# Halved conversion steps for the second matrix, scalars in early pieces, and the last reload moved, in a fused attention and two-layer kernel

## The chip, the cores and the metric

The kernel runs on one core of a Trainium2 chip. The metric is the device time of one execution in microseconds (us). Five engines work side by side, each through its own stream of instructions in order: TensorE (PE, and PEld for its weight loads), VectorE (DVE), ScalarE (ACT), GpSimd (POOL) and SyncE (SP), which here only issues transfers. They wait for each other through semaphores.

## The reference

Attention over 4 batches of 8 heads, 768 positions, head size 64, with a causal window of 128 and the first 4 positions kept for all; then two dense layers with a squared ReLU between them.

```python
scores = scale * np.matmul(q, k.transpose(0, 1, 3, 2))
rel = pos[:, None] - pos[None, :]
keep = (pos[None, :] < n_sink) | ((rel >= 0) & (rel < window))
scores = np.where(keep, scores, -1000000000.0)
a = np.exp(scores - np.max(scores, axis=-1, keepdims=True))
a = a / (np.sum(a, axis=-1, keepdims=True) + 1e-09)
x = np.matmul(a, v)          # as 3072 tokens x 512
h = x @ w_in                 # 512 -> 2048
r = np.maximum(h, 0.0)
g = s * (r * r) + b          # two scalars
out = g @ w_out              # 2048 -> 512
```

Two scalars, `s` and `b`, stand between the layers. [...]

## The kernel before

**Numbers.** Every operand of a matmul is held as a high part in TensorE's reduced 32-bit format and a low part, the difference; three products stand for one. A 64-bit value is read as two 32-bit words, and `float_steps` (L228) makes a 32-bit float of them: ScalarE scales the low word (L235) and the high word (L236), VectorE shifts the high word left by three into a scratch tile (L237), merges the sign (L239) and adds the low word (L241). Each works on 128 lanes x 1024 elements.

**Stages.** Tokens come in eight chunks of 384 (`CH`), each a half of a batch. The first stage computes attention for chunk 0 (`first_slots`) and converts the first matrix. Then comes a long list of steps of the first layer, 16 values of f per chunk in four pieces each (`l1_steps`, L678; L692 is its matmul, L698 its ReLU, L700 stores it to memory). Between these steps other work is placed: each entry of `todo` (L1056 to L1059) has a due time in units of f, and the loop takes out the entries that are due before it traces the next piece. `second_slots` is attention for the second chunk, `attn_slots` that of the other six: `unit_a` makes scores (L339, L340), the masked minimum on VectorE (L344) and the exponential on ScalarE (L350); `unit_b` transposes (L363, L364) and splits into high (L368, ScalarE) and low (L369, VectorE); `unit_c` and `unit_d` make the output and divide by the sum (L405, L432 to L438). One stage has all matmul outputs in eight PSUM banks, which come free when VectorE or ScalarE has read them.

**The second matrix** has eight blocks q (`NP`), each two rows of 128 x 512. The second layer uses a scheme with seven products of half blocks (`products`, L803; its matmul is L817), so a block needs seven matrices: three of its quarters and four sums, which `w2_steps` (L712) makes: `float_steps`, then subtractions into T (L718), `t0_t2` for two more of them, `low` for the quarters' high and low parts (L721 and L718), a copy of T in high form (L734, ScalarE) and the low form (L718, 128 x 1024). `tc.keep_in_program_order` pins an instruction's place among other pinned ones on its engine; the rest is ordered by a planner with its own costs. Six blocks are converted early: `early_w2` (L740) yields 12 steps per block, one of them the load of the next raw block, and they get due times spread evenly over 94 values of f. Three of these are written to memory and come back later through `reload` (L760), a transfer issued by POOL. The last two blocks are converted in the last chunk's first-layer stage (`late_w2`, L1077), in four calls each, and a reload follows each four; one call is taken per value of f.

**The second layer** has 48 units: six groups of 512 tokens times eight blocks. `load` brings the stored ReLU of one block on SP, `prep` squares it (L785), applies the scalars and forms the seven left operands (L787 to L798), `products` multiplies. The loop loads three units ahead and prepares one ahead.

**The scalars.** `scalars` (L190) works on single elements per lane: sign, scaled copies and a square root of |s| by four rounds of Newton's method (L205 to L208). It is due at t2 = 10.8, when attention for the second chunk is nearly done. Its results are first read by L236 of the second matrix's conversion.

Of the kernel before, what the change touches and what calls it, by code (L numbers as in the profile page):

```python
# [8 lines left out]
F32 = mybir.dt.float32  # L9
F32R = mybir.dt.float32r  # L10
I32 = mybir.dt.int32
U32 = mybir.dt.uint32
U8 = mybir.dt.uint8
AF = mybir.ActivationFunctionType
ALU = mybir.AluOpType
# [19 lines left out]
EARLY, SPILL = 3, 3  # L35
HD = DM // 2
NP = NF // 2
# [4 lines left out]
LB, LC, LD, L2, LEAD, PIECES = 3, 5, 2, 2, 2, 4  # L42
# [3 lines left out]
def tile_kernel(ctx, tc, qT, kT, k0, v, vsk, n_sink, window, w1, w2, s, b, out):  # L46
    nc = tc.nc
# [21 lines left out]
    def kept_v(q, name, shape, dt=F32):  # L69
        return kept.tile(shape, dt, tag=f"v{q}", name=name)  # L70

    def kept_raw(name, shape=(P, 2, 2 * DM), dt=I32):
        return kept.tile(list(shape), dt, tag="raw", name=name)
# [40 lines left out]
    rel, rel1, low, upp, kix, snk, tmp, tm2 = (sc0[:, j, :] for j in range(8))  # L114
# [73 lines left out]
    root_ap, b1_ap, b2_ap, sgn_ap, up_ap, abs_ap, t1_ap, t2_ap = (sbu[:, j:j + 1] for j in range(8))  # L188

    def scalars():  # L190


        ts = nc.vector.tensor_scalar
        stt = nc.vector.scalar_tensor_tensor
        tc.keep_in_program_order(ts(out=sgn_ap, in0=s_ap, scalar1=0.0, scalar2=2.0, op0=ALU.is_ge, op1=ALU.mult))
        ts(out=sgn_ap, in0=sgn_ap, scalar1=1.0, scalar2=None, op0=ALU.subtract)
        ts(out=up_ap, in0=sgn_ap, scalar1=2.0 ** -111, scalar2=None, op0=ALU.mult)
        stt(out=b1_ap, in0=b_ap, scalar=1 / WUP, in1=sgn_ap, op0=ALU.mult, op1=ALU.mult)
        ts(out=b2_ap, in0=b1_ap, scalar1=2.0, scalar2=None, op0=ALU.mult)
        nc.vector.tensor_tensor(out=abs_ap, in0=s_ap, in1=sgn_ap, op=ALU.mult)  # L200
        ts(out=abs_ap, in0=abs_ap, scalar1=1 / WUP, scalar2=1e-36, op0=ALU.mult, op1=ALU.max)
        ts(out=root_ap.bitcast(I32), in0=abs_ap.bitcast(I32), scalar1=1, scalar2=None, op0=ALU.logical_shift_right)
        ts(out=root_ap.bitcast(I32), in0=root_ap.bitcast(I32), scalar1=0x1fbd1df5, scalar2=None, op0=ALU.add)
        for _ in range(4):
            nc.vector.reciprocal(out=t1_ap, in_=root_ap)  # L205
            nc.vector.tensor_tensor(out=t2_ap, in0=t1_ap, in1=abs_ap, op=ALU.mult)
            nc.vector.tensor_tensor(out=t2_ap, in0=t2_ap, in1=root_ap, op=ALU.add)
            ts(out=root_ap, in0=t2_ap, scalar1=0.5, scalar2=None, op0=ALU.mult)  # L208

# [13 lines left out]
    def scratch(name, dt=F32):  # L225
        return kept.tile([P, 2, DM], dt, tag="cs", name=name, bufs=2)

    def float_steps(raw, scratch, pin=lambda x: x, up=2.0 ** -111):  # L228


        lo, hi = raw[..., 0], raw[..., 1]
        t = []
        sc, ve = nc.scalar, nc.vector
        return [
            lambda: pin(sc.activation(lo, lo.bitcast(U32), AF.Copy, scale=2.0 ** -29)),  # L235
            lambda: pin(sc.mul(hi.bitcast(F32), hi.bitcast(F32), up)),  # L236
            lambda: pin(ve.tensor_scalar(out=t.append(scratch()) or t[0], in0=hi, scalar1=3, scalar2=None,  # L237
                                         op0=ALU.logical_shift_left)),
            lambda: pin(ve.scalar_tensor_tensor(out=t[0], in0=hi, scalar=-0x80000000, in1=t[0],  # L239
                                                op0=ALU.bitwise_and, op1=ALU.bitwise_or)),  # L240
            lambda: pin(ve.tensor_tensor(out=hi, in0=t[0], in1=lo, op=ALU.add))]  # L241

    def to_float(raw, t):
        for f in float_steps(raw, lambda: t):
# [433 lines left out]
    def l1_steps(k, before):  # L678

        tk = slice(k.c * CH, (k.c + 1) * CH)  # L680
        g = {}

        order = [(cc, wi, 0) for cc in range(NCC) for wi in range(2)] + [(cc, 0, 1) for cc in range(NCC)]
        n = len(order) // PIECES

        def l1(f, piece):
            if piece == 0:
                before(f)
                g["h"] = po("h")
            h = g["h"]  # L690
            for i, (cc, wi, xi) in list(enumerate(order))[piece * n:(piece + 1) * n]:
                nc.tensor.matmul(h[:, :CH], w_in(f, wi)[:, cc * P:(cc + 1) * P], k.x[xi][:, cc, :],  # L692
                                 start=(i == 0), stop=(i == len(order) - 1))
            if piece < PIECES - 1:
                return
            if f % 2 == 0:
                g["r"] = kept.tile([P, 2, CH], F32, tag="g", name="g", bufs=3)
            nc.scalar.activation(g["r"][:, f % 2], h[:, :CH], AF.Relu, scale=1.0 / WUP)  # L698
            if f % 2 == 1:
                nc.sync.dma_start(gs[f // 2][:, :, tk], g["r"])  # L700

        return [lambda f=f, piece=piece: l1(f, piece) for f in range(NF) for piece in range(PIECES)]

    wc, raw2 = {}, {}
    spilled = {q: dram.tile([P, 7, 2, HD], F32R, tag=f"wd{q}", name=f"wd{q}") for q in range(EARLY, EARLY + SPILL)}

    def load_w2(q, raw=None):
        raw = kept_raw(f"vraw{q}") if raw is None else raw
        nc.sync.dma_start(raw, w2[q])
        raw2[q] = raw.rearrange("p c (f t) -> p c f t", t=2)  # L710

    def w2_steps(q):  # L712

        pin = tc.keep_in_program_order
        wb, wt = wc[q]
        v = raw2[q][..., 1].bitcast(F32)
        T = scratch("vT").rearrange("p c (h f) -> p (c h) f", h=2)
        sub = lambda o, x, y: pin(nc.vector.tensor_tensor(out=o, in0=x, in1=y, op=ALU.subtract))  # L718

        def low(o, x):  # L720
            pin(nc.scalar.copy(o[:, :, 0], x))  # L721
            sub(o[:, :, 1], x, o[:, :, 0].bitcast(F32))

        def t0_t2():
            sub(T[:, 2], v[:, 1, HD:], T[:, 1])
            sub(T[:, 0], T[:, 2], v[:, 1, :HD])

        o2 = T.rearrange("p (a c) f -> p c a f", c=2)[:, 1]
        return float_steps(raw2[q], lambda: scratch("vt", I32), pin, up_ap) + [
            lambda: sub(o2, v[:, :, HD:], v[:, 0].rearrange("p (h f) -> p h f", h=2)),  # L730
            t0_t2,
            lambda: low(wb[:, 0:2], v[:, :, :HD]),
            lambda: low(wb[:, 2:3], v[:, 1:2, HD:]),
            lambda: pin(nc.scalar.copy(wt[:, :, 0], T)),  # L734
            lambda: sub(wt[:, :, 1], T, wt[:, :, 0].bitcast(F32))]

    def halves_of(t):
        return t[:, :3], t[:, 3:]

    def early_w2():  # L740

        order = [(EARLY + j, j) for j in range(SPILL)] + [(q, q) for q in range(EARLY)]
        yield lambda: load_w2(order[0][0])
        for n, (q, tag) in enumerate(order):
            t = kept_v(tag, f"v{q}", [P, 7, 2, HD], F32R)
            wc[q] = halves_of(t)
            steps = w2_steps(q)
            if n + 1 < len(order):
                steps.insert(9, lambda: load_w2(order[n + 1][0]))
            yield from steps  # L750
            if q in spilled:
                nc.sync.dma_start(spilled[q].bitcast(F32), t.bitcast(F32))
# [290 lines left out]
            weights(NP - 1, (i - 20) // 2)  # L1043
    first_cm.__exit__(None, None, None)
    early = early_w2()
    n_early = 12 * (EARLY + SPILL)
    k2, plain = second_slots(ORDER[1])
    chunks = [k, k2] + [new_chunk(c) for c in ORDER[2:]]
    rows = attn_slots(chunks[2:])
    steps = [f for j, c in enumerate(chunks) for f in l1_steps(c, before if j == 0 else lambda f: None)]  # L1050
    n_last = (NC_ - 1) * NF

    t1 = NF / len(plain)
    t2 = H * BLK * t1 - LEAD
    dt = (n_last - LEAD - t2) / len(rows)
    todo = [(max(t * t1 - LEAD, 0.3), f) for t, f in enumerate(plain)] + [(t2 - 2, constants3), (t2, scalars)]  # L1056
    todo += [(t2 + t * dt, f) for t, f in enumerate(rows)]
    todo += [(NF + (t + 0.5) * (n_last - LEAD - NF) / n_early, lambda: next(early)()) for t in range(n_early)]
    todo.sort(key=lambda x: x[0])  # L1059
    n = 0  # L1060
# [13 lines left out]
    reload, load, prep, products, n_units = second_layer(p2)  # L1074
    late = {}

    def late_w2(q, a, z):  # L1077
        if a == 0:
            late[q] = w2_steps(q)
        for f in late[q][a:z]:  # L1080
            f()

    todo = []
    for j in range(2):
        todo += [lambda q=NP - 2 + j, a=a, z=z: late_w2(q, a, z) for a, z in ((0, 2), (2, 5), (5, 9), (9, 11))]
        todo.append(lambda j=j: reload(EARLY + 1 + j))
    for m in range(n, len(steps)):
        steps[m]()
        if m % PIECES < PIECES - 1:
# [1 line left out]
        m = m // PIECES - n_last  # L1091
# [7 lines left out]
    for n in range(n_units):  # L1099
        if n + 1 < n_units:  # L1100
            prep(n + 1)
        if n + 3 < n_units:
            load(n + 3)
        products(n)
    p2_cm.__exit__(None, None, None)
    kept_cm.__exit__(None, None, None)
# [49 lines left out]
```

## Time and profile before

| what | us |
| --- | --- |
| median of 3 runs | 728.08 (727.44 to 730.79) |
| profiled execution | 726.22 |
| its span | 724.5 |
| PE busy | 696.1 (96%) |
| PEld busy | 659.1 (91%) |
| DVE busy | 575.6 (79%) |
| ACT busy | 531.7 (73%) |
| POOL busy | 130.5 (18%) |

The span is what the profile covers; the execution's own time adds 1.7 us around it. A busy time is the time in which an engine has at least one instruction in work. Matmuls are pipelined, so a shown end lies behind the start of the next one; weight loads stand end to end when nothing holds TensorE up. The times of one kernel in different executions differ by a few tenths of a per cent.

### The profile page before, as it was taken

To read this page: it belongs to the slowest core of one execution; us is meant where nothing else is said; L and a number is where in the kernel's file an instruction comes from. 1 tells how busy PE (TensorE), PEld (TensorE's weight loads), DVE (VectorE), ACT (ScalarE), POOL (GpSimd) and SP (SyncE) were. 2 spreads that over 40 slices of the span, in tenths; PEclk is the share of its full clock that TensorE was granted. 3 is DMA by queue.
4 is the path that set the end of the run, shared out by engine and by line. 5 is a ranking of instruction groups with operands and counts; after the bars stand their busy time and mean duration, and the time that the engine had idled before them with its cause. 6 is when DMAs were issued, how large, how long until landed. Compare 5 with 4: busy or idle time off the path is not lost.

```text
span 724.5 us, 14198 instructions
## 1 busy us (share of the span) xinstructions
PE 696.1 (96%) x4858; PEld 659.1 (91%) x4858; DVE 575.6 (79%) x1458; ACT 531.7 (73%) x1229; POOL 130.5 (18%) x295
## 2 busy tenths in 40 slices
PE   9889999999999999999999999999999999999995
PEld 5667789999999998898899999999999999999995
DVE  7798976977887887877977862858888888888883
ACT  5898788789789789888888853846566665756561
POOL 4000122424424424424324310000000000000000
PEclk9999999999999999999999999999999999999998
DMA  8942254366456456453454318863534444443521
GB/s 206 410 148 84 67 180 149 107 209 219 133 178 222 141 169 244 126 175 112 136 185 131 108 67 327 267 221 117 154 109 124 138 118 146 117 146 117 151 84 62
DMA packets 61185, 114.13 MB, mean 158 GB/s; under 512 B 8368, under 2 KB 37168, under 8 KB 58288
## 3 DMA queue, kind: packets, MB, share of 16 engines
q1 hardware_dynamic: 59584, 107.43, 46.1%
q0 software_dynamic: 432, 5.51, 2.2%
q8 instruction: 40, 0.66, 0.4%
q14 instruction: 41, 0.34, 0.1%
q10 hardware_dynamic: 1088, 0.20, 0.1%
HBM read 76.16 MB, written 36.96 MB: 156 GB/s over the span
## 4 chain that ended last, share of the span: by engine, by line
PE 40%; DVE 14%; ACT 7%; DMA 7%; issue 4%; POOL 0%; ACTq 0%; DVEq 0%; POOLq 0%; SPq 0%
PE Q L817 21%; PE h L692 14%; DMA gs<-gs 5%; PE o L405 2%; DVE gA L796 2%; DVE sm L344 1%; DMA kraw<-in_kT 1%; ACT sm L350 1%; DVE hl L369 1%; ACT gs L785 1%; DVE gH L798 1%; DVE kl L321 1%; DVE u L830 1%; DVE qs L320 1%; ACT g L698 1%
## 5 line engine op out<-in xcount | busy, mean ns | idle before, releaser
L692 PE MATMUL h<-x,w 128*128 128x384 f32 x1536 | 306.4, 343 | 4.4 <-DVE negm L344 2.9
L692 PEld LDWEIGHTS h<-x,w 128*128 128x128 f32 x1536 | 261.9, 188 | 11.6 <-DVE negm L344 4.6
L817 PE MATMUL Q<-v,gH 128*128 128x256 f32 x1008 | 128.5, 283 | 0.3 <-DVE ot L830 0.2
L817 PEld LDWEIGHTS Q<-v,gH 128*128 128x128 f32 x1008 | 124.2, 192 | 0.7 <-issue 0.6
L785 ACT ACTIVATE gs<-gs,sbu 128x1024 f32<-128x1024 f32 x48 | 55.3, 1151 | 70.1 <-DMA gs<-gs 63.2
L817 PE MATMUL Q<-v,gA 128*128 128x256 f32 x756 | 99.0, 283 | 1.1 <-DVE gA L796 1.1
L350 ACT ACTIVATE sm<-sm,negm 128x264 f32<-128x264 f32 (+1 forms) x144 | 72.8, 506 | 32.3 <-DVE negm L344 28.8
L817 PEld LDWEIGHTS Q<-v,gA 128*128 128x128 f32 x756 | 94.4, 192 | 1.4 <-DVE gA L796 1.3
L698 ACT ACTIVATE g<-h 128x384 f32<-128x384 f32 x128 | 62.2, 490 | 18.6 <-PE h L692 13.3
L352 POOL COPY psk<-sm 128x24 f32<-128x24 f32 x144 | 37.0, 259 | 177.8 <-ACT sm L350 176.0
L369 DVE TENSOR_TENSOR hl<-tp,hl 128x256 fp32r<-128x256 f32 (+1 forms) x144 | 57.9, 403 | 9.7 <-ACT hl L368 8.7
L344 DVE CUSTOM_DVE_ANT_0 sm<-sc,msk 128x264 f32<-128x264 f32 (+1 forms) x144 | 59.0, 410 | 3.7 <-PE sc L340 1.2
L798 DVE TENSOR_TENSOR gH<-gs,gH 128x1024 fp32r<-128x1024 f32 x48 | 58.4, 1217 | 2.8 <-ACT gH L797 2.8
L795 ACT ACTIVATE gA<-gs,sbu 128x512 fp32r<-128x512 f32 x96 | 53.7, 607 | 8.3 <-PE Q L817 8.3
L405 PE MATMUL o<-hl,vv 128*128 128x128 f32 (+2 forms) x352 | 56.5, 278 | 3.4 <-DVE hl L369 1.7
L797 ACT CAST gH<-gs 128x1024 fp32r<-128x1024 f32 x48 | 50.0, 1041 | 12.1 <-DVE gs L790 7.0
L796 DVE SCALAR_TENSOR_TENSOR gA<-gs,sbu,gA 128x512 fp32r<-128x512 f32 x96 | 54.8, 611 | 0.0
L414 DVE TENSOR_TENSOR xm<-o,y 64x384 f32<-64x384 f32 x48 | 26.6, 555 | 34.3 <-ACT y L413 31.0
L787 DVE SCALAR_TENSOR_TENSOR gs<-gs,sbu 128x256 f32<-128x256 f32 x48 | 23.1, 482 | 37.9 <-ACT gs L785 37.7
L368 ACT CAST hl<-tp 128x256 fp32r<-128x256 f32 (+1 forms) x144 | 50.7, 353 | 1.7 <-PE tp L364 1.0
L405 PEld LDWEIGHTS o<-hl,vv 128*128 128x128 f32 (+1 forms) x352 | 40.3, 164 | 6.1 <-DVE hl L369 2.7
L339 PE MATMUL sc<-kh,qs 128*128 128x264 f32 (+1 forms) x144 | 40.2, 279 | 0.8 <-ACT g L698 0.6
(180 smaller groups left out, 1154.5 us busy)
## 6 DMA issues: line engine op xcount, KB each, us to landing
gs<-g SPq DMA_DIRECT2D x64, 384.0 KB, 3.1
gs<-gs SPq DMA_DIRECT2D x48, 512.0 KB, 4.2
kraw<-in_kT SPq DMA_DIRECT2D x32, 264.0 KB, 2.8
wraw<-in_w SPq DMA_DIRECT2D x8, 1024.0 KB, 11.4
vraw<-in_w SPq DMA_DIRECT2D x6, 1024.0 KB, 5.4
wd<-v SPq DMA_DIRECT2D x3, 1792.0 KB, 6.4
v<-wd POOLq DMA_DIRECT2D x3, 1792.0 KB, 9.5
out<-ot SPq DMA_DIRECT2D x10, 512.0 KB, 3.2
```

Source lines behind the costliest of these rows:

```text
L344: nc.vector.tensor_tensor_reduce(out=sm[:, :n], in0=sc[:, :n], in1=m, scale=-0.125, scalar=BIG, op0=ALU.add, op1=ALU.min, accum_out=negm[: ...
L350: nc.scalar.activation(sm[:, :n], sm[:, :n], AF.Exp, bias=negm[:, uu], scale=-1.0, accum_out=pp.zz[:, i, hh:hh + 1])
L368: nc.scalar.copy(hi, tp[:, a:z])
L369: nc.vector.tensor_tensor(out=lo, in0=tp[:, a:z], in1=hi.bitcast(F32), op=ALU.subtract)
L405: nc.tensor.matmul(hd.o[:m, q0:q0 + n * P], hd.vv[:, kb, :m], hd.hl[:, t, c0 * P:(c0 + n) * P], start=(hd.n == 0), stop=(end and t == 0))
L692: nc.tensor.matmul(h[:, :CH], w_in(f, wi)[:, cc * P:(cc + 1) * P], k.x[xi][:, cc, :], start=(i == 0), stop=(i == len(order) - 1))
L698: nc.scalar.activation(g["r"][:, f % 2], h[:, :CH], AF.Relu, scale=1.0 / WUP)
L785: nc.scalar.activation(g[:, 0], g[:, 0], AF.Square, scale=root_ap)
L795: nc.scalar.activation(o[:, :, 0], x, AF.Identity, bias=b1_ap, scale=1.0)
L796: stt(out=o[:, :, 1], in0=x, scalar=b1_ap, in1=o[:, :, 0].bitcast(F32), op0=ALU.add, op1=ALU.subtract)
L798: nc.vector.tensor_tensor(out=H[:, :, 1], in0=S, in1=H[:, :, 0].bitcast(F32), op=ALU.subtract)
L817: nc.tensor.matmul(bank[:, rb], left[j][:, gi, rb * P:(rb + 1) * P], right[j][:, wi], start=(q == 0 and (rb == 0 or parted) and i == 0), s ...
```

## The change

`float_steps` takes a number of parts: with two, both ScalarE steps, the merge and the add become two instructions on 512 elements each; the shift stays whole. In `w2_steps` the copy of T and its last subtraction are halved too, and `t0_t2` becomes two steps. A block then has 19 steps with the load (18 without) where it had 12, so `n_early` grows from 72 to 114 over the same due times; the load of the next raw block stays behind the second `low`. The four calls of `late_w2` per block cover the same work. `float_steps` for the first matrix keeps one part.

`scalars` loses Newton's rounds and becomes due 12 units of f earlier, which puts it ahead of all else in the list; four calls of `newton` follow at two units' distance, from t2 - 10 on. The last instruction of each is pinned.

The reload of block `EARLY + 1` keeps its place behind the first four late calls. The reload of `EARLY + 2`, which followed the last late call, is now traced in unit 0 of the second layer, after `prep(1)` and `load(3)`.

```diff
-        for _ in range(4):
-            nc.vector.reciprocal(out=t1_ap, in_=root_ap)
-            nc.vector.tensor_tensor(out=t2_ap, in0=t1_ap, in1=abs_ap, op=ALU.mult)
-            nc.vector.tensor_tensor(out=t2_ap, in0=t2_ap, in1=root_ap, op=ALU.add)
-            ts(out=root_ap, in0=t2_ap, scalar1=0.5, scalar2=None, op0=ALU.mult)
+
+    def newton():
+        ts = nc.vector.tensor_scalar
+        nc.vector.reciprocal(out=t1_ap, in_=root_ap)
+        nc.vector.tensor_tensor(out=t2_ap, in0=t1_ap, in1=abs_ap, op=ALU.mult)
+        nc.vector.tensor_tensor(out=t2_ap, in0=t2_ap, in1=root_ap, op=ALU.add)
+        tc.keep_in_program_order(ts(out=root_ap, in0=t2_ap, scalar1=0.5, scalar2=None, op0=ALU.mult))
...
-    def float_steps(raw, scratch, pin=lambda x: x, up=2.0 ** -111):
+    def float_steps(raw, scratch, pin=lambda x: x, up=2.0 ** -111, parts=1):
...
+        m = 2 // parts
+        cut = lambda x, j: x[:, j * m:(j + 1) * m]
+
+        def each(f):
+            return [lambda j=j: pin(f(cut(lo, j), cut(hi, j), j)) for j in range(parts)]
+
+        return (each(lambda l, h, j: sc.activation(l, l.bitcast(U32), AF.Copy, scale=2.0 ** -29)) +
+                each(lambda l, h, j: sc.mul(h.bitcast(F32), h.bitcast(F32), up)) +
+                [lambda: pin(ve.tensor_scalar(out=t.append(scratch()) or t[0], in0=hi, scalar1=3, scalar2=None,
+                                              op0=ALU.logical_shift_left))] +
+                each(lambda l, h, j: ve.scalar_tensor_tensor(out=cut(t[0], j), in0=h, scalar=-0x80000000, in1=cut(t[0], j),
+                                                             op0=ALU.bitwise_and, op1=ALU.bitwise_or)) +
+                each(lambda l, h, j: ve.tensor_tensor(out=h, in0=cut(t[0], j), in1=l, op=ALU.add)))
...
-        def t0_t2():
-            sub(T[:, 2], v[:, 1, HD:], T[:, 1])
-            sub(T[:, 0], T[:, 2], v[:, 1, :HD])
-
...
-        return float_steps(raw2[q], lambda: scratch("vt", I32), pin, up_ap) + [
+        two = (slice(0, 2), slice(2, 4))
+        return float_steps(raw2[q], lambda: scratch("vt", I32), pin, up_ap, 2) + [
             lambda: sub(o2, v[:, :, HD:], v[:, 0].rearrange("p (h f) -> p h f", h=2)),
-            t0_t2,
+            lambda: sub(T[:, 2], v[:, 1, HD:], T[:, 1]),
+            lambda: sub(T[:, 0], T[:, 2], v[:, 1, :HD]),
             lambda: low(wb[:, 0:2], v[:, :, :HD]),
-            lambda: low(wb[:, 2:3], v[:, 1:2, HD:]),
-            lambda: pin(nc.scalar.copy(wt[:, :, 0], T)),
-            lambda: sub(wt[:, :, 1], T, wt[:, :, 0].bitcast(F32))]
+            lambda: low(wb[:, 2:3], v[:, 1:2, HD:])] + [
+            lambda z=z: pin(nc.scalar.copy(wt[:, z, 0], T[:, z])) for z in two] + [
+            lambda z=z: sub(wt[:, z, 1], T[:, z], wt[:, z, 0].bitcast(F32)) for z in two]
...
-                steps.insert(9, lambda: load_w2(order[n + 1][0]))
+                steps.insert(14, lambda: load_w2(order[n + 1][0]))
...
-    n_early = 12 * (EARLY + SPILL)
+    n_early = 19 * (EARLY + SPILL)
...
-    todo = [...] + [(t2 - 2, constants3), (t2, scalars)]
+    todo = [...] + [(t2 - 2, constants3), (t2 - 12, scalars)] + [(t2 - 10 + 2 * j, newton) for j in range(4)]
...
-        todo += [lambda q=NP - 2 + j, a=a, z=z: late_w2(q, a, z) for a, z in ((0, 2), (2, 5), (5, 9), (9, 11))]
-        todo.append(lambda j=j: reload(EARLY + 1 + j))
+        todo += [lambda q=NP - 2 + j, a=a, z=z: late_w2(q, a, z) for a, z in ((0, 4), (4, 9), (9, 14), (14, 18))]
+    todo.insert(4, lambda: reload(EARLY + 1))
...
+        if n == 0:
+            reload(EARLY + 2)
         products(n)
```

## Rows read from the trace of the kernel before

**Rows 1.** The profile page's first line.

```profile
span 724.5 us, 14198 instructions
```

**Rows 2.** Windows by stage: length, then busy PE, PEld, DVE, ACT, POOL; clock, DMA.

```profile
44.00:106.00 62.00, 61.22 (x359) 48.92 (x358) 55.49 (x179) 52.44 (x141) 7.13 (x14) 1.00 0.37 125
106.00:434.00 328.00, 315.85 (x2092) 305.70 (x2091) 262.15 (x756) 274.68 (x774) 111.75 (x250) 1.00 0.48 155
434.00:471.00 37.00, 37.00 (x215) 36.72 (x214) 20.24 (x36) 21.76 (x36) 3.35 (x5) 1.00 0.85 291
471.00:724.50 253.50, 244.76 (x2026) 243.84 (x2025) 203.81 (x365) 149.14 (x193) 0.00 (x0) 0.99 0.42 129
```

**Rows 3.** TensorE's waits, 106 to 434 us: total us, times, longest.

```profile
PE h L692 <- DVE negm L344: 2.9, 5, 1.0
...
PE o L405 <- DVE hl L369: 1.7, 4, 0.6
```

**Rows 4.** Timeline from 295 us: start, us, instruction, idle before it and releaser.

```profile
295.63 1.23 DVE L239 SCALAR_TENSOR_TENSOR vt<-vraw,vt 128x1024 int32<-128x1024 int32 x1
...
297.38 0.19 PEld L434 LDWEIGHTS zb<-xsk,sel 128*128 128x128 f32 x1 [1.28 <-DVE negm L344]
```

**Rows 5.** Windows, six of 3.2 us from each L239's start, summed.

```profile
sum 19.20, PE 15.44 PEld 13.71 DVE 18.51 ACT 14.85 POOL 2.66; mean PE 2.57 PEld 2.28 DVE 3.08 ACT 2.47 POOL 0.44
```

**Rows 6.** Six 3.2 us windows from each last subtraction of T (L718), summed.

```profile
sum 19.20, PE 15.85 PEld 13.80 DVE 17.41 ACT 17.44 POOL 12.47; mean PE 2.64 PEld 2.30 DVE 2.90 ACT 2.91 POOL 2.08
```

**Rows 7.** Six 3.2 us windows from each L241, summed.

```profile
sum 19.20, PE 17.71 PEld 16.75 DVE 18.32 ACT 17.09 POOL 14.18; mean PE 2.95 PEld 2.79 DVE 3.05 ACT 2.85 POOL 2.36
```

**Rows 8.** Six 3.2 us windows from each L237, summed.

```profile
sum 19.20, PE 17.85 PEld 17.11 DVE 14.82 ACT 17.90 POOL 6.05; mean PE 2.97 PEld 2.85 DVE 2.47 ACT 2.98 POOL 1.01
```

**Rows 9.** Six 3.2 us windows from the first subtraction in each `t0_t2`, summed.

```profile
sum 19.20, PE 18.42 PEld 18.07 DVE 18.42 ACT 14.98 POOL 1.70; mean PE 3.07 PEld 3.01 DVE 3.07 ACT 2.50 POOL 0.28
```

**Rows 10.** Six 3.2 us windows from VectorE's part of each first `low`, summed.

```profile
sum 19.20, PE 18.49 PEld 17.47 DVE 14.31 ACT 15.46 POOL 5.64; mean PE 3.08 PEld 2.91 DVE 2.39 ACT 2.58 POOL 0.94
```

**Rows 11.** Six 3.2 us windows from each first subtraction into T, summed.

```profile
sum 19.20, PE 19.20 PEld 19.20 DVE 13.57 ACT 12.08 POOL 6.01; mean PE 3.20 PEld 3.20 DVE 2.26 ACT 2.01 POOL 1.00
```

**Rows 12.** Conversion steps by form, 106 to 434: count, busy, mean ns, idle.

```profile
L718 DVE TENSOR_TENSOR v<-vT,v 128x1024 fp32r<-128x1024 f32 x6 | 7.4, 1236 | 4.0 <-ACT v L734 4.0
L239 DVE SCALAR_TENSOR_TENSOR vt<-vraw,vt 128x1024 int32<-128x1024 int32 x6 | 7.4, 1226 | 0.2
...
L237 DVE TENSOR_SCALAR vt<-vraw 128x1024 int32<-128x1024 int32 x6 | 4.2, 695 | 3.2 <-ACT vraw L236 3.2
...
L718 DVE TENSOR_TENSOR vT<-vraw 128x512 f32<-128x512 f32 x6 | 4.1, 690 | 0.0
...
L235 ACT ACTIVATE vraw<-vraw 128x1024 int32<-128x1024 uint32 x6 | 6.8, 1136 | 0.1
...
L721 ACT CAST v<-vraw 128x512 fp32r<-128x512 f32 x6 | 4.0, 659 | 0.0
```

**Rows 13.** VectorE's timeline, first and last two of the 25 scalar instructions.

```profile
90.18 0.12 DVE L195 TENSOR_SCALAR sbu<-sb 128x1 f32<-128x1 f32 x1
...
98.48 0.15 DVE L207 TENSOR_TENSOR sbu<-sbu 128x1 f32<-128x1 f32 x1
98.67 0.15 DVE L208 TENSOR_SCALAR sbu<-sbu 128x1 f32<-128x1 f32 x1
```

**Rows 14.** POOL's timeline: the issue of the last reload.

```profile
468.71 0.53 POOL L763 DMA_DIRECT2D v<-wd  x1 [11.26 <-DVE vb L718]
```

**Rows 15.** The chain of waits: start, us, what; two loads of squares' inputs.

```profile
472.68 6.63 DMA gs<-gs
...
601.78 4.28 DMA gs<-gs
```

**Rows 16.** TensorE's waits, whole span: total us, times, longest.

```profile
PE Q L817 <- DVE gA L796: 1.1, 1, 1.1
...
PE sc L339 <- ACT g L698: 0.6, 1, 0.6
```

More of the change, by code (lines that the diff above doesn't have):

```diff
@@ L233, in float_steps @@
         sc, ve = nc.scalar, nc.vector
[L234 to L241, printed above, removed]
+        m = 2 // parts
[9 more added lines that the diff above has]
+                each(lambda l, h, j: ve.tensor_tensor(out=h, in0=cut(t[0], j), in1=l, op=ALU.add)))
     def to_float(raw, t):
@@ L1055, in tile_kernel @@
     dt = (n_last - LEAD - t2) / len(rows)
-    todo = [(max(t * t1 - LEAD, 0.3), f) for t, f in enumerate(plain)] + [(t2 - 2, constants3), (t2, scalars)]
+    todo = [(max(t * t1 - LEAD, 0.3), f) for t, f in enumerate(plain)] + [(t2 - 2, constants3), (t2 - 12, scalars)] + [(t2 - 10 + 2 * j, newton) for j in range(4)]
     todo += [(t2 + t * dt, f) for t, f in enumerate(rows)]
```

## The prediction

> **What bounds the kernel now.** I read the stages first [rows 1, 2]. Of 724.5 us, 328 (106 to 434 us) are the stage in which attention for six chunks, the first layer and the conversion of six blocks of the second matrix share the core. The reader should look at the third number there, the weight loads (PEld). Where TensorE never waits, loads stand back to back: 36.72 of 37.00 us from 434 to 471. In the mixed stage they fill 305.70 of 328.00, so TensorE loses 22.3 us. The plain PE number hides part of that (315.85), since a matmul's shown end covers a gap behind it. VectorE is busy 262.2 us (80%), ScalarE 274.7 (84%): neither is full, yet TensorE waits. The second layer after 471 runs at TensorE's own pace but for its start and its last drain, so only the mixed stage has something to give.
>
> The waits say on whom: L344's masked minimum and L369's low half, both on VectorE [rows 3]. A close look [rows 4] shows how: at 295.63 a conversion step, L239, holds VectorE for 1.23 us; the masked minimum runs behind it; the next weight load sits idle 1.28 us for it.
>
> So I summed the six windows of 3.2 us (19.2 us in all) that begin with each kind of conversion step on VectorE. PEld falls short of 19.20 by 5.49 us behind L239 [rows 5], 5.40 behind L718's last subtraction of T [rows 6], 2.45 behind L241 [rows 7], 2.09 behind L237 [rows 8], 1.13 behind the two subtractions of `t0_t2` [rows 9], 1.73 behind the first `low` [rows 10], and nothing behind the first subtraction into T [rows 11]: 18.3 of the 22.3 us. Durations sort them [rows 12]: the steps that cost most hold VectorE 1.23 us; the one that costs nothing takes 0.69. The last subtraction also made VectorE idle 4.0 us in all for its own ScalarE copy, and L237 3.2 us for L236.
>
> **The change part by part.** *Halved steps.* Per block three VectorE instructions (L239, L241, the last subtraction) and three of ScalarE (L235, L236, L734) become two each. Extra engine time over six blocks, with 512-element rows for the halves: VectorE 18 x (2 x 0.69 - 1.23) = 2.7 us, ScalarE 18 x (2 x 0.66 - 1.14) = 3.2 us [rows 12]. That lies in idle time (66 and 53 us of the stage). Steps come every 328/114 = 2.9 us instead of 328/72 = 4.6.
>
> What each half costs TensorE no row shows. Its lower bound is the first subtraction into T, as long as a half: 0. Its upper bound is the first `low`, which chains a 0.66 us ScalarE step and a 0.69 us VectorE step: 1.73/6 = 0.29 us. Below nothing it can't go. I take the middle, 0.15, so 12 halves of a kind cost 1.8 us. In kinds: L239 5.49 to 1.8; the last subtraction 5.40 to 1.8 (its copy now is a step or two ahead, so VectorE's wait goes as well); L241 2.45 to 1.8. L237 stays whole, but waits for half of L236 only: 0.53 + 0.70 us becomes 0.27 + 0.70, so 2.09 becomes about 1.6 (bounds 1.1 and 2.09). The two subtractions of `t0_t2`, now apart, are shorter than the step that costs nothing: 1.13 to 0 (bounds 0 and 1.13). Together 16.6 becomes 7.0: 9.6 us fewer. With every half at its bounds it is between 3.0 and 15.5.
>
> Not all of it stays. What is late next is ScalarE: its free time in the stage was 328 - 274.7 = 53.3 us, and a stage shorter by g with 3.2 us more work leaves 50.1 - g. As an estimate I let the remaining waits (22.3 - 9.6 = 12.7 us) grow as this free time shrinks: 12.7 x 53.3/(50.1 - g) = 22.3 - g gives g = 6.7 us. The same with the bounds gives 1.2 and 12.6. I take 6.7.
>
> [...] The rows show VectorE at 80% over the stage [rows 2] but 18.51 of 19.20 us (96%) in the windows behind L239 [rows 5]. [...]
>
> *Scalars.* Twenty-five instructions of one element per lane leave VectorE's stream at 90.2 to 98.8 us, where a dependent pair starts 0.19 us apart, about 0.2 [rows 13]. They go ahead of the second chunk's first unit, and Newton's four rounds 2, 4, 6 and 8 units f later, at 328 us for 94 f some 3.5 us each, so all before 75 us. Gain where they were: TensorE's only wait behind them in the list is one of 0.6 us, L339 for L698's output [rows 16], so 0 to 0.6 us. Cost where they go: none if they fall into VectorE's 6.5 free us of the 62 from 44 to 106 [rows 2], and at most 25 x 0.20 = 5.0 us if each holds up the chain of a softmax. Most are short pieces between others, so I take 0 net. If the cover is gone, TensorE waits for L612's or L258's output there.
>
> *The last two blocks' steps* run in the stage from 434 to 471, where the loads lose 0.28 us of 37 [rows 2]. Nothing to win; the extra 6 + 6 instructions are hidden by the 17 and 15 free us of the two engines. 0.
>
> *The last reload.* Its transfer is issued by POOL, which waits for one thing, the last read of the raw block by L718, and starts at 468.71 [rows 14]. SP's loads are another queue. In the program the reload moves behind a load on SP and two preparations, but nothing in POOL's stream stands between, so I expect it at the same point: 0. If it did move behind the load of unit 3, that load (6.63 us at 472.68, against 4.28 for a later one [rows 15]) would be free of it, and TensorE's one wait of 1.1 us for `gA` [rows 16] might go, which is the upper bound. Its block is first read by unit 5, some 26 us on (48 units in 253.5 us [rows 2]), so lateness costs nothing.
>
> Sum: 726.2 us (the profiled execution, 724.5 and 1.7 around it) - 6.7 = 719.5. The runs shown have a median 1.9 us above the profiled execution, so the timed forecast is **721.4 us**.
>
> **The rivals.** *1, the slower side: halves that stall twice.* The windows behind L239 have VectorE at 96%; when the second half comes 2.9 us after the first, the backlog of the first may still stand, and the masked minimum comes late twice. The 18 whole steps cost 13.3 us, 0.74 each; the change loses as soon as a half costs over 0.37. At 0.5 it is 36 x 0.5 - 13.3 = +4.7: 732.8 us. For it: 42 more steps in the same streams, and places that shift. Against it: the first subtraction into T [rows 11]. A split costs VectorE 2 x 0.69 - 1.23 = 0.15 us by rows 12. [...]
>
> *2, scalars in a full place.* If the 25 instructions delay the second chunk by their 5.0 us, 721.4 + 5.0 = 726.4. For it: VectorE 55.5 of 62 us there. Against it: ScalarE and TensorE are the later ones in part of it, and Newton's pieces stand apart.
>
> *3, the gain doesn't stay.* At the lower end, 1.2 us: 726.9. For it: ScalarE at 84%, and `ACT` waits and VectorE waits that chase each other. Against it: the windows behind the first subtraction into T, where a step of 0.69 us costs nothing [rows 11].
>
> **How the numbers follow.** Forecast 0.57, rival 1 0.13, rival 2 0.13, rival 3 0.17. A difference under 0.5%, 3.6 us, can't be told from none. Faster by more (below 724.4): the forecast and a little of rivals 2 and 3, 0.59. Within: the rest of these two, 0.28. Slower (above 731.7): rival 1, 0.13. The range: down to 716, most of the upper end of the stage's gain (728.1 - 12.6 = 715.5), up to 730 to hold rivals 2 and 3 and the mild part of 1.
>
> **What would show it.** Right: the same 305.7 us of weight loads in a mixed stage of about 321 us; twelve windows each behind the halves of L239 and of the last subtraction that lose under 2.5 us in all; VectorE's wait for L734 gone; the second layer as long as before. Wrong: the 18 us lost still there with other releasers, the time from 44 to 106 longer by more than 1 us, or a reload that starts elsewhere than at the last L718 of the raw block.

## The result, and the profile after

The changed kernel takes 732.39 us (median of 16 runs, 730.18 to 734.75); the kernel before takes 727.72 us on the same chip. The ratio of their runs is 1.0056 (95% interval 1.0043 to 1.007; the two medians alone would give 1.0064): slower by 0.56%, where 721.4 us was forecast.

The page's first line and the windows of the four stages (length, then busy PE, PEld, DVE, ACT, POOL; clock, DMA share, GB/s) answer to [rows 1, 2].

```profile
span 729.3 us, 14225 instructions
```

```profile
44.00:106.00 62.00, 58.32 (x330) 44.57 (x329) 51.99 (x168) 49.95 (x131) 5.68 (x11) 1.00 0.33 110
106.00:434.00 328.00, 319.61 (x2107) 308.67 (x2106) 262.72 (x782) 280.52 (x800) 111.84 (x252) 0.99 0.49 157
434.00:471.00 37.00, 37.00 (x215) 36.72 (x214) 17.72 (x34) 19.15 (x36) 3.26 (x4) 1.00 0.79 276
471.00:729.30 258.30, 247.50 (x2043) 246.54 (x2041) 209.76 (x377) 153.78 (x202) 0.53 (x1) 0.99 0.42 130
```

The mixed stage does what was hoped for, in part: its weight loads fill 308.67 of 328 us, 3.0 more than before. But the stage ahead of it lost 4.4 us of loads (44.57 after 48.92), and the second layer begins later than it should. To see where, I noted when TensorE starts the same matmul in both traces. The last column is experiment e9 below, the same change with six loads of a megabyte put in another order, at three places.

| TensorE starts | before | after | after - before | e9 - before |
| --- | --- | --- | --- | --- |
| first layer, matmul 0 | 40.31 | 41.28 | +0.97 | +2.06 |
| matmul 192 | 107.17 | 111.51 | +4.34 | +2.25 |
| matmul 480 | 193.74 | 195.91 | +2.17 | -0.46 |
| matmul 576 | 221.28 | 226.03 | +4.75 | -0.92 |
| second layer, unit 0 | 472.57 | 475.36 | +2.79 | -2.23 |
| unit 3 | 489.06 | 494.44 | +5.38 | -1.58 |
| end | 724.46 | 729.26 | +4.80 | -2.75 |

The first row is start-up, which the change doesn't touch (in the control e13, where only the reload's call is moved, it is +3.57). Behind it three jumps, +3.4, +2.6 and +2.6 us, stand against two stretches that gain 2.2 and 2.0.

**First jump.** SyncE's issues, before and then after: the first raw load of the second matrix (`vraw`, 1024 KB) and the key load that follows it.

```profile
89.36 0.39 SPq L709 DMA_DIRECT2D vraw<-in_w  x1
...
92.50 0.33 SPq L298 DMA_DIRECT2D kraw<-in_kT  x1
```

```profile
93.67 0.57 SPq L716 DMA_DIRECT2D vraw<-in_w  x1
94.83 0.33 SPq L305 DMA_DIRECT2D kraw<-in_kT  x1
```

These two key loads in the list of issues (size, time to landing), before and after:

```profile
kraw<-in_kT SPq DMA_DIRECT2D x1, 264.0 KB, 3.1
```

```profile
kraw<-in_kT SPq DMA_DIRECT2D x1, 264.0 KB, 7.9
```

Then the timeline after, at 103 us:

```profile
102.74 0.63 ACT L326 CAST kh<-kraw 128x528 fp32r<-128x528 f32 x1 [1.74 <-DMA kraw<-in_kT]
...
103.40 0.71 DVE L328 TENSOR_TENSOR kl<-kraw,kh 128x528 fp32r<-128x528 f32 x1 [1.94 <-ACT kh L326]
...
104.03 0.55 DVE L659 TENSOR_TENSOR x<-o,x 128x384 fp32r<-128x384 f32 x1
...
104.72 0.36 PE L346 MATMUL sc<-kh,qs 128*128 128x264 f32 x1 [2.98 <-DVE x L659]
```

Read it upwards: TensorE waits 2.98 us for the second chunk's `x`, which stands on VectorE behind the low half of the keys, which waits for ScalarE's high half, which waits for a transfer. That one was issued 1.16 us behind a megabyte instead of 3.14. (A store of 384 KB, issued at 92.44, stands ahead of it too; before, it stood behind, at 92.92.) In the trace the raw load's 128 packets of 8192 bytes start between 95.62 and 100.04 us, the key load's 128 of 2112 bytes between 98.40 and 102.19: it was issued at 94.83, and its first packet starts 3.57 us later.

**Second jump**, the same picture with the third raw load (issued at 210.21, a store of 384 KB at 210.85; a key load of 200 KB at 211.87 lands 6.7 us later, before 2.4 us):

```profile
218.64 0.53 ACT L326 CAST kh<-kraw 128x400 fp32r<-128x400 f32 x1 [2.03 <-DMA kraw<-in_kT]
...
219.61 0.47 PE L370 MATMUL tp<-identr,sm 128*128 128x128 f32 x1 [1.97 <-ACT g L705]
```

The three windows around it show a second price, the clock that TensorE was granted around the end of the wait (0.51, half speed):

```profile
215.60:219.00 3.40, 1.70 (x9) 1.17 (x8) 1.29 (x5) 1.34 (x5) 0.39 (x2) 1.00 0.50 166
219.00:222.40 3.40, 2.79 (x12) 2.79 (x13) 2.44 (x9) 2.37 (x9) 0.97 (x3) 0.51 0.47 148
222.40:226.00 3.60, 3.60 (x25) 3.60 (x24) 3.51 (x7) 3.55 (x12) 2.36 (x4) 0.99 0.22 67
```

**Third jump.** SyncE again, before and after: the two late raw loads (1024 KB each) and a store of the first layer's output (`gs<-g`).

```profile
435.74 0.51 SPq L700 DMA_DIRECT2D gs<-g  x1
436.43 1.03 SPq L709 DMA_DIRECT2D v<-in_w  x2
```

```profile
438.91 0.81 SPq L716 DMA_DIRECT2D v<-in_w  x2
439.77 0.53 SPq L707 DMA_DIRECT2D gs<-g  x1
```

They changed places. The ReLU that needs the stored buffer free waits 5.96 us for that store (before: 2.11 at 450.51), the late conversion on the same engine starts late, and the load of unit 3 goes out 2.9 us behind unit 0's start instead of 0.1 [rows 15]:

```profile
452.54 0.49 ACT L705 ACTIVATE g<-h 128x384 f32<-128x384 f32 x1 [5.96 <-DMA gs<-g]
```

```profile
478.30 0.57 SPq L783 DMA_DIRECT2D gs<-gs  x1
```

All 16 traces of this case show what that place costs. From unit 0 to unit 1 it is 5.03 us in the eleven where the store goes first and 6.07 to 6.43 in the five where the raw loads do (the change, e1, e5, e7, e10).

**The reload** starts at the same event as before [rows 14]:

```profile
473.92 0.53 POOL L768 DMA_DIRECT2D v<-wd  x1 [11.27 <-DVE vb L725]
```

### The profile page after: what moved, and what is told of

It is laid out like the page before. It is cut to its first block, busy times and chain, and to the rows that moved or that the text cites. A ratio compares the mean times of both kernels' runs of the same rounds, so it can differ in the third digit from the quotient of the medians.

```text
span 729.3 us, 14225 instructions
## 1 busy us (share of the span) xinstructions
PE 698.3 (96%) x4858; PEld 659.7 (90%) x4858; DVE 575.2 (79%) x1482; ACT 536.2 (74%) x1253; POOL 129.5 (18%) x295
## 4 chain that ended last, share of the span: by engine, by line
PE 65%; DVE 12%; ACT 9%; DMA 8%; issue 4%; POOL 0%; SPq 0%; DVEq 0%; ACTq 0%; POOLq 0%
PE Q L822 31%; PE h L699 20%; PE o L412 3%; DMA kraw<-in_kT 2%; DMA gs<-g 2%; PE sc L347 1%; PE tp L370 1%; PE sc L346 1%; PE tp L371 1%; DMA q<-in_qT 1%; DVE sm L351 1%; ACT sm L357 1%; DVE hl L376 1%; DMA wraw<-in_w 1%; ACT g L705 1%
## 5 line engine op out<-in xcount | busy, mean ns | idle before, releaser
L359 POOL COPY psk<-sm 128x24 f32<-128x24 f32 x144 | 39.4, 274 | 186.8 <-ACT sm L357 186.1
L412 PE MATMUL o<-hl,vv 128*128 128x128 f32 (+2 forms) x352 | 58.0, 280 | 1.6 <-DVE hl L376 1.2
## 6 DMA issues: line engine op xcount, KB each, us to landing
v<-wd POOLq DMA_DIRECT2D x3, 1792.0 KB, 10.8
```

Of the source, the lines that this page charges most:

```text
L412: nc.tensor.matmul(hd.o[:m, q0:q0 + n * P], hd.vv[:, kb, :m], hd.hl[:, t, c0 * P:(c0 + n) * P], start=(hd.n == 0), stop=(end and t == 0))
```

## The experiments

Theory A: the halves gain, and the change loses through the order of transfers at the three places. Rival: halves and scalars cost in themselves. Each kernel was timed beside the kernel before (726.65, 727.52, 726.88 or 727.68 us in the four groups), so ratios are compared. "Stage" is the time from the first layer's matmul 96 to the second layer's unit 0: 396.5 us before, 398.9 in the changed kernel.

### Parts of the change

**Halves alone** (e1): the change without the scalars' and the reload's move.

> The halved conversion steps alone (19 steps a block, scalars and last reload as before). Theory A, three separate places: the changed kernel loses 4 us at 92 to 112 us through the scalars' move, loses 2.6 us at 445 to 490 us because the two late raw loads now stand ahead of one store in SP's stream, and gains some 3 us between through the halves. Then this kernel has no loss at 92 to 112, the gain of about 3 us and still the loss of 2.6 us at the second layer's start: 0 to -1.5 us against the kernel before. Rival B, halves cost in themselves (more steps, each in the way once): this kernel is slower by 3 us or more, with the loss spread over 106 to 434 us.

Ratio 1.0026 (1.0007 to 1.0045), 729.06 us: neither theory's time. The second and third jumps are there, the first isn't; TensorE waits 2.00 us until 216.48 with 3.41 us of half clock behind it. Theory A had no second jump in it; B's loss over the whole stage isn't there either (the stage is 1.4 us shorter than before).

**Scalars alone** (e2).

```diff
-    todo = [...] + [(t2 - 2, constants3), (t2, scalars)]
+    todo = [...] + [(t2 - 2, constants3), (t2 - 12, scalars)] + [(t2 - 10 + 2 * j, newton) for j in range(4)]
...
```

> The scalars in early pieces alone (whole conversion steps, last reload as before). Theory A: the first load of the second matrix goes out later and directly ahead of a key load, and TensorE waits some 3 to 5 us around 105 us: slower by 3 to 4.5 us, the stage after it and the start of the second layer as in the kernel before. Rival B: within 1 us of the kernel before.

Ratio 1.0055 (1.0037 to 1.0072), 731.68 us, 4.0 us by the ratio, as A said: this part by itself costs as much as the whole change. The first jump is +4.9 us between matmuls 96 and 192.

**The reload alone** (e13): its call moved behind `prep(1)` and `load(3)`.

> The last reload's place in the program alone. The prediction (POOL waits for the last read of the raw block, nothing else in its stream stands between): the reload starts right behind that read as before, 727 to 728 us, ratio 0.998 to 1.002. Rival (it goes out behind the load of the fourth unit, which then lands in some 4.5 us instead of 6.6): the 1.1 us wait for the left operand goes, 726 us.

Ratio 0.9992 (0.9976 to 1.0007). It starts where it did, at the last read of the raw block:

```profile
471.21 0.53 POOL L763 DMA_DIRECT2D v<-wd  x1 [11.28 <-DVE vb L718]
```

### The order of the transfers

**Late raw loads behind the store** (e4), in the changed kernel. The two loads and the store change places in SyncE's stream; no other instruction moves.

```diff
-                nc.sync.dma_start(gs[f // 2][:, :, tk], g["r"])
+                last["store"] = nc.sync.dma_start(gs[f // 2][:, :, tk], g["r"]).ins
...
-            load_w2(NP - 2 + q, late_v(EARLY + 1 + q, [P, 2, 2 * DM], I32))
+            with tc.issue_after(last["store"]):
+                load_w2(NP - 2 + q, late_v(EARLY + 1 + q, [P, 2, 2 * DM], I32))
...
+    steps[n]()
+    n += 1
     wk_cm.__exit__(None, None, None)
```

> The changed kernel with one thing altered: in SP's stream the two late raw loads stand behind the store of the first layer's output that they stood ahead of (all engines' other instructions in the same order). Theory A: ScalarE's wait of 6 us for a store at 446 to 452 us shrinks to about 2 us, the load of unit 3 goes out within 0.5 us of the second layer's first matmul instead of 2.8 us after it, and TensorE's waits in the first units of the second layer fall from 3.2 to about 1.2 us: 2 to 2.6 us faster than the changed kernel. Rival B: no difference over 0.7 us. A second rival, that the last reload's move does it: no difference either, since the reload is where it was.

Ratio 1.003 (1.0016 to 1.0045): 0.26%, 1.9 us, less than the change. The ReLU's wait falls to 1.78 us; the load of unit 3 goes out 1.3 us behind unit 0, not 0.5. **The same on halves alone** (e8):

> Halves alone, with only the two late raw loads put behind the first-layer store; all else as in halves alone. Theory A (the place of these two loads costs the start of the second layer 2.6 to 3.2 us, as it did in the changed kernel): 725.5 to 726.5 us, ratio about 0.998. Rival (the store's place matters only together with the scalars' move): as halves alone, 729 us.

0.9985 (0.9968 to 1.0003), 0.41% less than e1, as A said. The third place is shown twice. Two more pairs with the same edit come below: e6 against e7 gains nothing, e14 against e10 0.22%, less than the noise.

**First raw load behind the next two key loads** (e5), in the changed kernel.

```diff
...
+        last.setdefault("kraw", []).append(nc.sync.dma_start(hd.k[:, :hd.kw], kT[k.b, h, :, hd.k0:hd.k0 + hd.kw]).ins)
...
-        yield lambda: load_w2(order[0][0])
+        def first_load():
+            with tc.issue_after(last["kraw"][-2]):
+                load_w2(order[0][0])
+
+        yield first_load
```

> The changed kernel with the first load of the second matrix (1 MB) placed behind the next two key loads in SP's stream, no longer in front of them. Theory A: the key load that landed 8 us after its issue lands in some 3 us, the waits of 3.0 us and 2.0 us of TensorE around 105 us go, 3 to 4 us faster than the changed kernel. Rival, the moved scalars' own instructions hold VectorE: no gain over 1 us, and the waits stay with VectorE as releaser though the keys are there.

Ratio 1.0024 (1.0005 to 1.0043): 0.32%, 2.3 us, less, under the 3 to 4 expected. The key load lands in 4.4 us, and 0.9 us of the 3.0 us wait stay. The planner answered the edit by moving a few conversions and copies of the second chunk on the other engines as well, here and in e12. **The same on scalars alone** (e12):

> The scalars' move alone, with the first raw load of the second matrix behind the next two key loads (102 us instead of 94). Theory A (the move costs through that load alone): 727 to 728.5 us, ratio 0.999 to 1.002, TensorE's 2.6 us wait for x of the second chunk down to about 1 us. Rival (the 25 instructions themselves hold up VectorE's conversion of the first matrix and the second chunk): 730 us or more, ratio 1.003 or above.

1.0019 (0.9999 to 1.0039), 0.36% less than e2, as A said. The wait at 104 us shrinks, but something stays:

```profile
PE sc L341 <- DVE x L654: 0.9, 1, 0.9
```

How much, the stretch from matmul 96 to 192 tells, which the start-up's differences don't touch: 31.0 to 31.1 us in all ten traces without the scalars' move, 34.6 to 36.0 with it (the change, e4, e2), 32.9 to 33.0 with the first raw load put behind the keys as well (e5, e9, e12). So the load's place costs 1.6 to 3.1 us there, and 1.9 us stay. Whether these are the scalars' own instructions or the store that still stands ahead of the key load, no run separates.

**Early raw loads behind their key loads** (e7), on halves alone: the load of raw blocks 2, 3 and 5, counted from 0, is traced right behind the next key load. A few instructions of the other engines follow in another order.

```diff
-        nc.sync.dma_start(hd.k[:, :hd.kw], kT[k.b, h, :, hd.k0:hd.k0 + hd.kw])
+        keys = nc.sync.dma_start(hd.k[:, :hd.kw], kT[k.b, h, :, hd.k0:hd.k0 + hd.kw]).ins
+        if behind_keys:
+            with tc.issue_after(keys):
+                load_w2(behind_keys.pop())
...
-                steps.insert(14, lambda: load_w2(order[n + 1][0]))
+                steps.insert(14, lambda: (behind_keys.append if n + 1 in (2, 3, 5) else load_w2)(order[n + 1][0]))
```

> Halves alone, with only the early raw loads put behind the key loads; the two late raw loads still go out ahead of the store. Theory A: the 2.0 us wait for keys at 217 us and the half-clock stretch behind it (1.7 us of matmul pace) go, so 2.5 to 4 us less than halves alone: 725 to 726.5 us, ratio about 0.998. Rival (the wait for keys is made up before the next wait, so taking it away gives nothing): as halves alone, 729 us, ratio 1.0026.

Ratio 0.9959 (0.9944 to 0.9975), 724.88 us: 0.67% less than e1, more than expected. No half clock at 217 us, no wait of 2 us; the key loads there land in 3.0 to 3.3 us. Halves alone are now clearly faster than the kernel before. The mixed stage:

```profile
106.00:434.00 328.00, 321.61 (x2120) 309.98 (x2119) 263.11 (x779) 279.65 (x797) 113.94 (x253) 1.00 0.48 156
```

**Both orders on halves alone** (e6: e7 and e8 together).

> Halves alone, with SyncE's order mended at two places: the raw loads of the second matrix that stood directly ahead of a key load (the second early one, at 207 us, and two later ones) go out directly behind that key load, and the two late raw loads go out behind the first-layer store as in the kernel before. Theory A (the halves save about 5 us in the mixed stage, and the change loses time through the order of the transfers alone): ratio to the kernel before 0.992 to 0.997 (721 to 724.5 us), no ScalarE wait of 2 us for keys at 217 us, first unit q0 at 2 to 4 us earlier than before, unit boundary q126 no longer later than before. Rival B (halves cost in themselves in what they add of instructions): 727 us or more, ratio 1.000 or above. Rival C (a TensorE that runs ahead meets the next late transfer, so the gain is lost elsewhere): 725 to 727 us, with a new wait of 1.5 us or more at another place.

0.9958 (0.9942 to 0.9974): no better than e7. Unit 0 is 1.99 us early, but by unit 3 that is gone, in a TensorE wait of 1.50 us for `gA` and half clock at 483.58 to 486.99 us. So rival C holds for the last step, and the two repairs don't add up in time.

**The whole change with all three orders mended** (e9).

> The whole change, with SyncE's order mended at all three places: first raw load behind the next two key loads, three raw loads behind their key loads, two late raw loads behind the store. Theory A (the scalars' move costs only through the raw load that it moves ahead of a key load, and what VectorE is held up itself is 1 to 2 us): 723 to 726.5 us, ratio 0.994 to 1.000. Rival (the scalars' own instructions hold VectorE where its conversions end last, 3 to 5 us): 727 us or more, with the first lost 3 us at 92 to 107 us still there.

Ratio 0.996 (0.9941 to 0.9979), 723.68 us: 0.96%, 7.0 us less than the change as it stands, with the same halves, scalars and reload. A's range holds, with the 1.9 us above for what stays at the first place; the rival's 727 us does not. Its first two stages:

```profile
44.00:106.00 62.00, 60.69 (x347) 47.27 (x347) 53.36 (x173) 51.35 (x136) 5.85 (x12) 1.00 0.34 115
106.00:434.00 328.00, 321.82 (x2121) 310.34 (x2120) 263.86 (x783) 280.02 (x797) 113.47 (x253) 1.00 0.49 157
```

### Which halves gain

**VectorE's halves alone** (e10), on e7: ScalarE's three steps stay whole, with an empty step behind each.

```diff
-            lambda z=z: pin(nc.scalar.copy(wt[:, z, 0], T[:, z])) for z in two] + [
+            lambda: pin(nc.scalar.copy(wt[:, :, 0], T)), lambda: None] + [
...
```

> As halves with the keys in order, but only VectorE's steps are halved; ScalarE's three steps per block stay whole, with an empty step behind each so that due times stay. In the profile of halves with keys in order, the windows of 3.2 us behind VectorE's merge lost 4.5 us (5.5 before), behind the last subtraction 3.7 (5.4), behind the add 1.0 (2.5), behind the pair of subtractions 1.1 (1.1 before), behind the shift 0.8 (2.1). Theory A (each step's gain is its own engine's): the first four kinds keep their gain, the shift's falls away: some 3 us of the 4.3 in the mixed stage stay, 725.5 to 726.5 us. Rival (the gain comes through ScalarE's halves, since VectorE's wait for whole copies is what is late): at most 1 us stays, 727.5 us or more, and the merge's halves lose 5 us or more again.

Ratio 0.9967 (0.9949 to 0.9986), 724.81 us. The stage is 6.1 us shorter than before, against 4.2 with both halved (e7): more, not less. The windows behind the last subtraction lose 0.8 us (3.7 with both halved), and those behind the shift 2.1 as before, as A said of the shift. The start of the second layer gives the gain back (21.2 us from unit 0 to unit 3, 16.5 before).

**ScalarE's halves alone** (e11), the other side.

> The other side: only ScalarE's three steps per block are halved, VectorE's stay whole. Theory A: the windows behind the shift gain 1 to 1.5 us, the others stay as before (5.5, 5.4, 2.5 us): 727 to 728.5 us, ratio about 1.000. Rival: most of the 4.3 us of the mixed stage stay, 725 to 726 us.

0.9974 (0.9957 to 0.9992), 724.87 us; the stage is 2.6 us shorter. Theory A missed this: the windows behind the last subtraction fell too, from 5.4 us lost to 2.4. By time alone e7, e10 and e11 can't be told apart. Nor are e10 and e11 quite alike: in e11 the two late raw loads stay behind the store unasked (a store at 433.6 us, the loads at 434.3 and 434.8), so its like is e14 below.

The traces tell more. VectorE's groups for the halves of the last subtraction, e7 and then e10 (count, busy, mean ns, idle before and releaser):

```profile
L728 DVE TENSOR_TENSOR v<-vT,v 128x512 fp32r<-128x512 f32 x12 | 10.4, 868 | 3.6 <-ACT v L742 3.6
```

```profile
L730 DVE TENSOR_TENSOR v<-vT,v 128x512 fp32r<-128x512 f32 x12 | 8.3, 689 | 0.0
```

and VectorE's waits for ScalarE's high half of the keys, e7 and e10 (total, times, longest):

```profile
DVE kl L331 <- ACT kh L329: 4.9, 6, 1.5
```

```profile
DVE kl L333 <- ACT kh L331: 1.5, 5, 0.6
```

With ScalarE's steps halved, VectorE waits 3.6 us for the copy of T, and 4.9 instead of 1.5 us for the keys.

**The copy whole again** (e15), on e6.

> As halves of both engines with both orders mended, but ScalarE copies T whole again, with an empty step behind it. Theory A (the first half of the last subtraction waits for the second half of the copy, which is traced just ahead of it; with the whole copy a step earlier the wait goes): VectorE's wait for the copy under 0.5 us instead of 3.6, the twelve windows behind the last subtraction's halves lose about 0.7 us instead of 3.7, and the mixed stage gains 1.5 to 2.5 us more: 722.5 to 723.5 us. Rival (the copy's halves are harmless and the other halves of ScalarE, those of the two scalings, take the gain back): 724.7 us as with both halved.

Ratio 0.9944 (0.9923 to 0.9965). The wait for the copy is gone and the windows behind the last subtraction lose 0.8 us instead of 3.7, as A said; but the stage is 4.2 us shorter than before, as e6's 4.1. What these windows gained went elsewhere, 0.6 us of it behind the shift; A's "1.5 to 2.5 us more" is refuted, and by time e15 and e6 can't be told apart.

**VectorE's halves alone with both orders** (e14): e10 with e4's edit.

> As VectorE's halves alone with the keys in order, but the two late raw loads go out behind the first-layer store; two lines of SyncE's order change places, nothing else. Theory A (that place costs the start of the second layer about 2 us): 722 to 723.5 us, ratio 0.993 to 0.9955, the faster of all versions. Rival (an earlier TensorE only meets the next late transfer): as before this edit, 724.8 us, ratio 0.9967.

Ratio 0.9945 (0.9925 to 0.9965), 723.78 us, stage 5.5 us shorter, unit 3 at -3.68. With e15 the lowest ratio, 0.55% below the kernel before.

## Why the prediction was wrong

**The sign.** Forecast -6.7 us, measured 0.56% of 727.7 = +4.1; 10.8 us lie between. 7.0 of them are the order of the transfers at three places (e9 against the change; 5 to 9 by the intervals). The other 3.8 are the halves' smaller gain with the rest, the 1.9 us that stay at the first place among it. Part of the 7.0 is clock: the granted clock averages 0.9907 over the 16 runs of the change, 0.9951 over the 8 of e9 and 0.9950 over the 29 of the kernel before timed beside e1. As an estimate from these, that is at most 0.0044 x 728 = 3.2 us, about two stretches of 3.41 us at half clock per run. No term and no rival of mine named the order of the transfers; rival 2 had the right place with another mechanism, rival 1's sign came without its mechanism.

**The scalars (0 net) are the step that failed first.** I weighed 25 short instructions against VectorE's 6.5 free us, and looked at who waits for L258. I did not ask what is issued when L258 is done: the first raw load, which takes the last first-matrix block's buffer. In the changed trace that block's last step starts at 90.17 us instead of 87.09 (start-up makes 0.97 of it), and the first raw load goes out directly ahead of a key load. As the bound 0 to 5.0 us the price was inside, but the value taken was that of the free time. Scalars alone cost 0.55%; with the load behind the keys 0.19%, an interval that touches zero. The sign I gave myself, "the time from 44 to 106 longer by more than 1 us", came true (+3.37 us from matmul 0 to 192).

**The due times of the early steps: no term at all.** "Steps come every 2.9 us instead of 4.6" was counted for VectorE only. One of a block's 19 steps is a load of a megabyte, and with new due times it stands elsewhere among the key loads: 0.67% (e1 to e7).

**The last two blocks (0).** "Nothing to win" was right for the engines. But the two raw loads there went ahead of a store: 0.26% (e4), 0.41% (e8).

**The halves (6.7 us): right mechanism, wrong size.** The stage gained 4.1 to 4.2 us with both engines halved and the keys in order (e6, e7). In e9's trace, windows as in [rows 5 to 9], in us lost:

| steps | before | forecast | e9 |
| --- | --- | --- | --- |
| merge, halves | 5.49 | 1.8 | 4.35 |
| last subtraction, halves | 5.40 | 1.8 | 3.68 |
| add, halves | 2.45 | 1.8 | 0.91 |
| shift, whole | 2.09 | 1.6 | 0.59 |
| first of the pair | 1.13 | 0 | 0.77 |

A half of the three kinds costs 8.94/36 = 0.25 us, not 0.15: within the bounds of 0 and 0.29, near the upper one, and under the 0.37 at which rival 1 would have won. The sign I gave, twelve windows each that lose under 2.5 us in all, failed with 4.35 and 3.68. (The windows of two halves overlap a little, so the sums are slightly high.) The five kinds fell by 6.3 us, not 9.6. The last step of the working, that 6.7 of 9.6 stay, did hold: in e9's mixed stage the loads fill 4.6 us more than before (310.34 after 305.70). Though VectorE is at 96% behind L239 [rows 5], kernels with its steps halved were faster than before: e7 (0.9959) and e10 (0.9967).

**"VectorE's wait for L734 gone": wrong.** It was 4.0 us [rows 12] and is 3.1:

```profile
DVE v L725 <- ACT v L739: 3.1, 5, 0.8
```

The changed kernel's timeline of one block:

```profile
159.13 0.62 ACT L739 CAST v<-vT 128x512 fp32r<-128x512 f32 x1
...
164.59 0.62 ACT L739 CAST v<-vT 128x512 fp32r<-128x512 f32 x1
...
165.24 1.08 DVE L725 TENSOR_TENSOR v<-vT,v 128x512 fp32r<-128x512 f32 x1 [0.68 <-ACT v L739]
...
168.17 0.68 DVE L725 TENSOR_TENSOR v<-vT,v 128x512 fp32r<-128x512 f32 x1
```

The first subtraction needs only the first copy, 6 us old, yet runs right behind the second. I had counted the copy "a step or two ahead" by the first half.

**Right:** the reload (0; same releaser, control 0.9992), and the second layer's pace once started (unit 3 to the end 235.4 us before, 234.8 after).

**Open:** why ScalarE's halves shorten the windows behind VectorE's whole last subtraction (e11) and yet add nothing to VectorE's halves. All runs with halves, e11 too, have the new due times with them; none has these with every step whole, so how much of the gain is the wider spacing isn't shown.

**The start of the second layer** has a second spread, and the traces name it. From unit 0 to unit 3 it is 16.5 us in the profile before and 18.6 in the control, which does the same work in the same order but had 3.41 us of half clock from 487.19 on. Over the 16 traces, with the store first: 16.5 to 17.8 us at full clock (seven), 18.6 to 19.3 with such a stretch (four). With the raw loads first: 19.1 at full clock (the change), 19.8 to 21.2 with it (four). So some 2 us there come and go with the clock between single executions, beside what the order costs.

## What to carry to other kernels

When steps with due times are split or moved, list every transfer among them and what stands next to it in its queue before and after; here a small load that lands behind a large one cost more than the moved instructions can have (0.36% by e2 and e12, against the 0.19% left). A free-time account of the engines can't see this. After a change that loses, mend the order of transfers before dropping the idea: here the same change went from +0.56% to -0.40%.

## What the runs showed of the hardware

- A key load of 264 KB issued 3.14 us behind a load of 1024 KB landed in 3.1 us; issued 1.16 us behind it, with a store of 384 KB ahead of both, in 7.9 us. For 200 KB: 2.4 us at 4.07 us behind, 6.7 us at 1.66 us behind with such a store between.
- TensorE's granted clock fell from 1.00 to 0.50 for 3.41 us in or just behind a wait of about 2 us, at 216 to 223 us in the changed kernel, e1, e4 and e8; in e5 a wait of 2.32 us at the same place brought none. At 483 to 494 us it fell in eight of the 16 traces, the control among them; seven others, with a wait of 1.5 us at the same place, had none. As an estimate from these, such a stretch cost up to 1.7 us (half of 3.41) beyond the wait itself; it didn't come in every execution.
- A half of the last subtraction took 0.67 us with no GpSimd instruction beside it (at 225.30 us), and 1.08 to 1.15 us where GpSimd's `x` had started 0.40 to 0.47 us ahead. GpSimd's timeline in the changed kernel, beside the two subtractions at 165.24 and 168.17 us:

```profile
164.77 1.01 POOL L445 TENSOR_TENSOR x<-xm,x 128x384 fp32r<-128x384 f32 x1 [0.64 <-ACT x L444]
...
168.15 1.58 POOL L445 TENSOR_TENSOR x<-xm,x 128x384 fp32r<-128x384 f32 x1 [0.43 <-ACT x L444]
```

  In the first pair the subtraction is the long one, 1.08 us beside an `x` of 1.01. In the second, where `x` starts 0.02 us ahead (0.08 at 389.77 us), `x` is: 1.58 us (1.64) beside a subtraction of 0.68. What decides which of the two takes longer isn't shown. The halved copy set the first subtraction right behind the `x` of GpSimd; in e10, with ScalarE's steps whole, the twelve halves took 0.69 us on average, in e7 0.87.
